# Loading pair 0's q on another queue, moving constant fills off VectorE, and reordering one FFN tile in a fused attention + FFN kernel

## The chip, the cores and the metric

The kernel runs on one core of one Trainium2 chip. The metric is the device time of that core in microseconds (us), from runs without the profiler unless a profiled run is named. The span in a profile is 1.7 to 1.8 us shorter than the time of the same execution.

## The reference

```python
# q, k, v: [8, 8, 576, 64]; x = attention out, [4608, 512]; d_ff = 1536
q_d, k_d, v_d = mean of q, k, v over groups of 4 positions        # 144 positions
out_up    = repeat(softmax(q_d k_d^T / 8) v_d, 4)                 # coarse, upsampled
out_local = softmax(q k^T / 8 where |i - j| < 4) v                # banded
x   = (out_up + out_local).transpose(0, 2, 1, 3).reshape(4608, 512)
out = (relu(x @ w_gate) * (x @ w_val)) @ w_out
```

## The kernel before

The program walks through 32 *pairs* of heads. For a pair it transposes q and k, computes scores (`emit_s1`), takes the exponential on ScalarE, multiplies by the band masks on VectorE, multiplies with v, and writes the normed result, transposed, into `xT`. Four *lead-in* pairs (0 to 3) come first, because the FFN contracts over four pairs. Then 36 *slots* follow: each does one third of an FFN chunk's hidden tiles (`emit_h`) and, for as long as there are any, one more pair. TensorE runs dummy matmuls (`emit_warm`) where it would otherwise stand still in the lead-in.

Constant fills, all on VectorE ahead of its other work:

```python
    nc.vector.memset(zero_sb, 0.0)
    nc.vector.memset(ones_sb[:, 0:64], 1.0)
    nc.vector.memset(ones_sb[:, 64:128], 4.0)
    for t in vw:                                   # 7 buffers, 112 x 768 each
        nc.vector.memset(t[:, :, 64:128], 1.0)
    for t in vd:
        nc.vector.memset(t[:, :, 64:128], 4.0)
    # ... then small fills of qkT (4), ee (2), ed (2), xo (3)
```

The loads of the first nine pairs go through GpSimd's queue and change fp32 into fp16 on the way:

```python
        for src, dst in ((q, qk16[r][:, 0, :]), (k, qk16[r][:, 1, :])):
            if hp < NTP:
                nc.gpsimd.dma_start(dst..., _dap(src, off, ...))
```

The transposes of pairs 0 to 8 are 24 small matmuls into three PSUM banks, q's 12 first, k's 12 after. ScalarE copies the first two banks out, VectorE the third:

```python
        for n in range(2 * NB):                    # 0..5: q, 6..11: k
            bank = b0 if n < 4 else b1 + n // 4 - 1
            for hh in range(2):
                nc.tensor.matmul(out=ps[64 * hh : 64 * hh + 64, bank, lo : lo + 120],
                                 lhsT=sv[:, n // NB, hh, n % NB, :], rhs=eyesum_sb, ...)
        for i, bank in enumerate((b0, b1, b1 + 1)):
            if i < 2:
                nc.scalar.copy(...)                # pooled part, then full part
            else:
                nc.vector.tensor_copy(...)
```

The mask product and the x sum have both inputs in SBUF; so have the additions on GpSimd that pool v over four positions, needed from pair 9 on:

```python
            nc.vector.tensor_tensor(out=o, in0=o, in1=masks..., op=ALU.mult)     # emit_s1
        nc.vector.tensor_tensor(out=xT[...], in0=x[...], in1=x[...], op=ALU.add) # emit_xsum
        nc.gpsimd.tensor_tensor(out=m, in0=t[...], in1=t[...], op=ALU.add)       # emit_vd_pool
        nc.gpsimd.tensor_tensor(out=o..., in0=m[...], in1=m[...], op=ALU.add)    # emit_vd_pool
```

The first FFN slot and the order of a slot's first steps:

```python
    def emit_slot(s, gate):
        c, jj, hp = s // 4, 3 * (s % 4), s + LEAD
        if NVP <= hp + 1 < NP:
            emit_vd_pool(hp + 1)                   # GpSimd, from slot 4 on
        emit_in(hp + 4)                            # GpSimd issues loads
        # ...
        if s == 0:
            emit_qkT_pe(hp, 2, 3)
            emit_warm(2)
            emit_x_pe(hp - 1, 0)                   # pair 3's x into xT
            emit_warm(1)
        # ... then emit_h(c, jj, 0): eight matmuls over all four pairs of xT
```

And the head of the program:

```python
        nc.sync.dma_start(cst_sb, cst_dr)          # masks, identity and so on
        for hp in range(4):
            emit_in(hp)
        emit_warm(10)
        emit_qkT_pe(0, 2, 3)
        emit_warm(4)
        for hp in range(LEAD):
            emit_fill(hp)
```

The softmax here doesn't subtract the row's maximum and nothing guards it: scores larger than these inputs give would overflow.

## Time and profile before

| | before |
|---|---|
| time, median of 3 runs | 358.13 us (358.11 to 358.15) |
| span of the profiled execution | 357.1 us (its time was 358.89, 0.8 above the timed ones) |
| TensorE busy | 349.9 us, 98% |
| q / k of pair 0 land | 5.50 / 6.44 us |
| first exponential | 9.36 us |

The page's first part gives busy time, share and number of instructions of each engine.

```profile
PE 349.9 (98%) x2855; PEld 178.5 (50%) x2855; DVE 227.3 (64%) x338; ACT 212.4 (59%) x366; POOL 187.7 (53%) x231
```

TensorE has next to no idle time to give. The view by stretch shows where the little is; its columns are the length of the stretch, then each engine's busy time with its instruction count, TensorE's granted clock, DMA share and GB/s.

```profile
0.00:10.00 10.00, 8.21 (x61) 3.73 (x62) 7.27 (x26) 3.16 (x7) 8.91 (x14) 1.00 1.58 128
10.00:27.00 17.00, 15.86 (x294) 11.24 (x293) 15.04 (x37) 12.27 (x33) 13.92 (x17) 1.00 2.12 170
```

"Busy" is padded by dummy matmuls, so the lead-in can still be shortened. The timeline of the first 14 us says how. Columns: start, duration, engine, line, operation, output<-input, shapes, count, and in brackets how long the engine stood idle before and what ended that.

```profile
1.26 4.45 PE L557 MATMUL ps<-zero_sb 128*128 128x512 f16 x10 [1.26 <-DVE zero_sb L130]
...
5.63 1.66 PE L214 MATMUL ps<-cst_sb,qk_0_75 96*64 96x120 f16 x24
...
6.30 0.70 DVE L134 MEMSET vw_95<- 112x768 f16 x1
...
7.22 1.04 PE L557 MATMUL ps<-zero_sb 128*128 128x512 f16 x4
...
8.09 0.17 DVE L144 MEMSET xo_111<- 32x128 uint32 x1
8.28 0.26 DVE L229 CAST qkd_100<-ps 128x96 f16<-128x96 f32 x1
...
8.46 0.55 DVE L230 CAST qkT_96<-ps 128x384 f16<-128x384 f32 x1
...
9.36 1.19 ACT L283 ACTIVATE ee_102<-ps 112x576 f16<-112x576 f32 x2 [1.81 <-PE ps L274]
```

VectorE is still filling constants until 8.25 us. The last transposes of pair 0 end at 7.29, but the copies of the third bank do not start before 8.28.

The same view around slot 0:

```profile
25.38 0.61 PE L557 MATMUL ps<-zero_sb 128*128 128x512 f16 x2
...
25.98 0.28 PE L444 MATMUL ps<-cst_sb,xo_109 72*128 72x288 f16 x1
...
26.48 0.38 PE L557 MATMUL ps<-zero_sb 128*128 128x512 f16 x1
...
26.88 1.02 PE L468 MATMUL ps<-xT,wg_sb 128*128 128x512 f16 x4
```

Three dummies surround pair 3's x transposes; then come the eight matmuls of the first hidden tile, until 28.7.

### The profile page before, as it was taken

What the parts mean: (1) busy time and instruction counts of PE and PEld (TensorE: products, weight loads), DVE (VectorE), ACT (ScalarE), POOL (GpSimd) and SP (SyncE); (2) the same over time, 40 slices, a digit from 0 to 9 for tenths busy, and PEclk for the clock granted to TensorE, in tenths of its full rate; (3) what the DMA queues carried; (4) which work ended last, traced back from release to release, by engine and by line L of the source; (5) the groups of instructions that cost most, each with busy time, mean ns of one, the idle gap of its engine ahead of it and who ended that gap; (6) DMA issues with size and microseconds to landing.
All of it is one profiled execution on the core that took longest, in us unless ns stands there. A gap on an engine that the chain in (4) does not pass through costs nothing.

```text
span 357.1 us, 7235 instructions
## 1 busy us (share of the span) xinstructions
PE 349.9 (98%) x2855; PEld 178.5 (50%) x2855; DVE 227.3 (64%) x338; ACT 212.4 (59%) x366; POOL 187.7 (53%) x231
## 2 busy tenths in 40 slices
PE   8999999999999999999999999999999999999996
PEld 3665555545455455555555555554445444444443
DVE  8793666586786877788887788776675432232220
ACT  2766776667777666666666666666776532322321
POOL 8976547999999877767678877722000000000000
PEclk9999999999999999999999999999999999999999
DMA  9999999999999999999999999950000110000022
GB/s 125 165 172 187 182 194 155 166 159 178 169 173 138 159 169 130 132 132 131 133 125 130 124 123 133 117 108 28 21 20 23 44 46 30 31 29 29 31 59 89
DMA packets 166882, 40.11 MB, mean 112 GB/s; under 512 B 149728, under 2 KB 162240, under 8 KB 166848
## 3 DMA queue, kind: packets, MB, share of 16 engines
q0 software_dynamic: 134128, 23.07, 85.8%
q1 hardware_dynamic: 27520, 7.27, 16.2%
q10 hardware_dynamic: 5200, 9.31, 7.7%
q8 instruction: 22, 0.36, 0.4%
q14 instruction: 12, 0.10, 0.1%
HBM read 46.45 MB, written 9.44 MB: 157 GB/s over the span
## 4 chain that ended last, share of the span: by engine, by line
PE 90%; DVE 5%; ACT 2%; issue 1%; DVEq 0%
PE ps L468 51%; PE ps L490 25%; PE ps L408 3%; PE ps L274 2%; PE ps L416 2%; PE ps L214 2%; PE ps L263 2%; DVE xn_114 L386 1%; PE ps L520 1%; ACT rden_112 L385 1%; ACT rden_112 L383 1%; DVE xT L391 1%; PE ps L347 1%; PE ps L247 0%; PE ps L317 0%
## 5 line engine op out<-in xcount | busy, mean ns | idle before, releaser
L468 PE MATMUL ps<-xT,wg_sb 128*128 128x512 f16 x432 | 110.9, 379 | 0.8 <-DVE xn_114 L386 0.5
L468 PE MATMUL ps<-xT,wv_sb 128*128 128x512 f16 x432 | 110.9, 379 | 0.0
L490 PE MATMUL ps<-wo_sb,gT 128*128 128x512 f16 x420 | 100.1, 380 | 0.0
L468 PEld LDWEIGHTS <-wv_sb 128*128 128x128 f16 x432 | 42.2, 98 | 51.1
L468 PEld LDWEIGHTS <-wg_sb 128*128 128x128 f16 x432 | 39.8, 97 | 44.3 <-issue 1.0
L490 PEld LDWEIGHTS <-gT 128*128 128x128 f16 x420 | 39.0, 98 | 45.6
L498 ACT COPY y_sb<-ps 128x512 f32<-128x512 f32 x35 | 20.5, 587 | 46.9 <-PE ps L490 46.9
L432 DVE TENSOR_TENSOR xn_115<-ps,rden_113 64x720 f16<-64x720 f32 x24 | 21.7, 905 | 22.4 <-ACT rden_113 L429 22.1
L432 DVE TENSOR_TENSOR xn_114<-ps,rden_112 64x720 f16<-64x720 f32 x22 | 19.9, 905 | 20.1 <-ACT rden_112 L429 19.8
L283 ACT ACTIVATE ee_102<-ps 112x576 f16<-112x576 f32 x32 | 19.1, 648 | 14.6 <-PE ps L274 14.0
L283 ACT ACTIVATE ee_103<-ps 112x576 f16<-112x576 f32 x32 | 19.1, 648 | 12.5 <-PE ps L274 12.3
L426 ACT ACTIVATE rden_113<-ps 64x720 f32<-64x720 f32 x24 | 18.4, 765 | 7.1 <-PE ps L416 6.8
L286 DVE TENSOR_TENSOR ee_102<-ee_102,cst_sb 112x576 f16<-112x576 f16 x32 | 20.7, 682 | 2.6 <-ACT ee_102 L283 2.4
L426 ACT ACTIVATE rden_112<-ps 64x720 f32<-64x720 f32 x22 | 16.8, 764 | 6.2 <-PE ps L416 5.9
L286 DVE TENSOR_TENSOR ee_103<-ee_103,cst_sb 112x576 f16<-112x576 f16 x32 | 18.4, 615 | 0.0
L391 DVE TENSOR_TENSOR xT<-xn_114 128x576 f16<-128x576 f16 x14 | 13.0, 932 | 0.1
L557 PE MATMUL ps<-zero_sb 128*128 128x512 f16 x33 | 11.4, 457 | 1.3 <-DVE zero_sb L130 1.3
L391 DVE TENSOR_TENSOR xT<-xn_115 128x576 f16<-128x576 f16 x14 | 11.1, 795 | 0.1
L292 ACT ACTIVATE ed_104<-ps 72x576 f16<-72x576 f32 x16 | 10.3, 643 | 0.0
L292 ACT ACTIVATE ed_105<-ps 72x576 f16<-72x576 f32 x16 | 10.3, 643 | 0.0
L429 ACT ACTIVATE rden_113<-rden_113 128x720 f32<-128x720 f32 x12 | 9.6, 803 | 0.4
L235 POOL TENSOR_TENSOR vd_106<-v_0_87 72x256 f16<-72x256 f32 x4 | 2.9, 720 | 12.2 <-PE ps L416 12.1
(463 smaller groups left out, 602.4 us busy)
## 6 DMA issues: line engine op xcount, KB each, us to landing
out_dram<-y_sb ACTq DMA_DIRECT2D x34, 256.0 KB, 4.0
wg_sb<-in_moe_w_gate_dram POOLq DMA_DIRECT2D x4, 384.0 KB, 10.0
wv_sb<-in_moe_w_val_dram POOLq DMA_DIRECT2D x4, 384.0 KB, 10.4
wo_sb<-in_moe_w_out_dram POOLq DMA_DIRECT2D x4, 384.0 KB, 11.8
vw_90<-in_v_dram POOLq DMA_DIRECT2D x5, 168.0 KB, 6.0
vw_91<-in_v_dram POOLq DMA_DIRECT2D x5, 168.0 KB, 5.9
vw_92<-in_v_dram POOLq DMA_DIRECT2D x5, 168.0 KB, 6.6
v_4_86<-in_v_dram POOLq DMA_DIRECT2D x5, 144.0 KB, 7.2
```

The costliest lines, as they stand in the source:

```text
L283: nc.scalar.activation(out=o, in_=ps[0:WK, p0 + 2 * g : p0 + 2 * g + 2, 0:288], func=AF.Exp, scale=scale)
L286: nc.vector.tensor_tensor(out=o, in0=o, in1=_sap(masks_sb, (0, WK), 288 * g, [[0, 2], [1, 288]]), op=ALU.mult,)
L292: nc.scalar.activation(out=ed[r2][:, :, 0 : 2 * SD].rearrange("p h (c t) -> p c h t", c=2), in_=ps[0:72, p0 : p0 + 4, 288:432].rearrange(" ...
L391: nc.vector.tensor_tensor(out=xT[:, kk, b * S : (b + 1) * S].rearrange("p (c t f) -> p c t f", c=2, f=4), in0=x[:, :, 0:288].rearrange("p ...
L408: nc.tensor.matmul(out=ps[:, bank, NQ * j : NQ * j + NQ], lhsT=vflat[:, v0 : v0 + 128], rhs=e[:, hh, lo : lo + NQ], start=True, stop=True,)
L426: nc.scalar.activation(out=r[lo : lo + 64], in_=ps[de : de + 64, 4 + 2 * hh : 6 + 2 * hh, 0:360], func=AF.Ln)
L429: nc.scalar.activation(out=r, in_=r, func=AF.Exp, scale=-1.0)
L432: nc.vector.tensor_tensor(out=x[lo : lo + 64], in0=ps[lo : lo + 64, 4 + 2 * hh : 6 + 2 * hh, 0:360], in1=r[lo : lo + 64], op=ALU.mult,)
L468: nc.tensor.matmul(out=h, lhsT=w[:, kk, bass.ts(jj, 128)], rhs=xT[:, kk, c * TCH : (c + 1) * TCH], start=(kk == 0), stop=(kk == 3),)
L490: nc.tensor.matmul(out=y_ps, lhsT=gts[c, jj][:, bass.ts(ty, 128)], rhs=wo_sb[:, jj, :], start=(jj == 0), stop=(jj == NJJ - 1),)
L498: nc.scalar.copy(out=y_sb, in_=y_ps)
L557: nc.tensor.matmul(out=ps[:, 7, :], lhsT=zero_sb[:, 0:128], rhs=zero_sb[:, 128:640], start=True, stop=True)
```

## The change

There are three intents. (a) Load pair 0's q as fp32 through SyncE's queue and cast it on ScalarE, so that k can take q's place in GpSimd's queue, and transpose k first. (b) Take fills out of VectorE's way: three `vw` fills to GpSimd, the small ones behind the first copies. (c) In slot 0 replace the dummies with the part of the first hidden tile that needs only pairs 0 to 2, and give that slot other PSUM banks.

```diff
@@ -130,18 +131,20 @@
     nc.vector.memset(zero_sb, 0.0)
     nc.vector.memset(ones_sb[:, 0:64], 1.0)
     nc.vector.memset(ones_sb[:, 64:128], 4.0)
-    for t in vw:
+    for t in vw[0:4]:
         nc.vector.memset(t[:, :, 64:128], 1.0)
-    for t in vd:
-        nc.vector.memset(t[:, :, 64:128], 4.0)
     for t in qkT:
 ...
-    for t in ed:
-        nc.vector.memset(t[:, :, 2 * SD :], 0.0)
-    for t in xo:
-        nc.vector.memset(t[64:96, NB:, :], 0.0)
+
+    def emit_pads():
+        for t in ee:
+            nc.vector.memset(t[:, :, S:], 0.0)
+        for t in ed:
+            nc.vector.memset(t[:, :, 2 * SD :], 0.0)
+        for t in vd:
+            nc.vector.memset(t[:, :, 64:128], 4.0)
+        for t in xo:
+            nc.vector.memset(t[64:96, NB:, :], 0.0)
 
     def pair(i):
         return ps[:, 2 * i : 2 * i + 2, :]
@@ -154,7 +157,13 @@
         r = hp % NL
         b, off = head_off(hp)
         for src, dst in ((q, qk16[r][:, 0, :]), (k, qk16[r][:, 1, :])):
-            if hp < NTP:
+            if hp == 0 and src is q:
+                nc.sync.dma_start(
+                    q32.rearrange("p (n d) -> p n d", d=64),
+                    _dap(src, off, [[D, 96], [NQ * D, 2 * NB], [1, D]]),
+                )
+                nc.scalar.copy(out=dst, in_=q32)
+            elif hp < NTP:
                 nc.gpsimd.dma_start(
@@ -207,7 +216,10 @@
     def emit_qkT_pe(hp, b0, b1):
         r, r4, r2 = hp % NL, hp % 4, hp % 2
         sv = qk16[r].rearrange("p i (h j d) -> p i h j d", h=2, d=64)
-        for n in range(2 * NB):
+        blocks = list(range(2 * NB))
+        if hp == 0:
+            blocks = blocks[NB:] + blocks[:NB]
+        for n in blocks:
 ...
@@ -220,14 +232,18 @@
                 )
         big = qkT[r4][:, 0 : 2 * S].rearrange("p (b n t) -> p b n t", b=3, n=4)
         sml = qkd[r2].rearrange("p i t -> p (i t)").rearrange("p (b n t) -> p b n t", b=3, n=4)
-        for i, bank in enumerate((b0, b1, b1 + 1)):
+        act, dve = nc.scalar.copy, nc.vector.tensor_copy
+        if hp == 0:
+            plan = ((2, 1, act), (2, 0, act), (1, 1, dve), (1, 0, dve), (0, 1, act), (0, 0, dve))
+        else:
+            plan = ((0, 1, act), (0, 0, act), (1, 1, act), (1, 0, act), (2, 1, dve), (2, 0, dve))
+        for i, pooled, copy in plan:
+            bank = b0 if i == 0 else b1 + i - 1
             t = ps[:, bank, 0:480].rearrange("p (n t) -> p n t", n=4)
-            if i < 2:
-                nc.scalar.copy(out=sml[:, i], in_=t[:, :, 96:120])
-                nc.scalar.copy(out=big[:, i], in_=t[:, :, 0:96])
+            if pooled:
+                copy(out=sml[:, i], in_=t[:, :, 96:120])
             else:
-                nc.vector.tensor_copy(out=sml[:, i], in_=t[:, :, 96:120])
-                nc.vector.tensor_copy(out=big[:, i], in_=t[:, :, 0:96])
+                copy(out=big[:, i], in_=t[:, :, 0:96])
 
     def emit_vd_pool(hp):
         t, m, o = v4[hp % NV4], v2[hp % 2], vd[hp % 3]
@@ -461,17 +477,21 @@
 
     gts = {}
 
-    def emit_h(c, jj, pp):
+    def emit_h_mm(c, jj, pp, which, kks):
+        w = (wg_sb, wv_sb)[which]
+        for kk in kks:
+            nc.tensor.matmul(
+                out=pair(pp)[:, which, :],
+                lhsT=w[:, kk, bass.ts(jj, 128)],
+                rhs=xT[:, kk, c * TCH : (c + 1) * TCH],
+                start=(kk == 0),
+                stop=(kk == 3),
+            )
+
+    def emit_h(c, jj, pp, parts=((0, range(4)), (1, range(4)))):
         h1, h2 = pair(pp)[:, 0, :], pair(pp)[:, 1, :]
-        for w, h in ((wg_sb, h1), (wv_sb, h2)):
-            for kk in range(4):
-                nc.tensor.matmul(
-                    out=h,
-                    lhsT=w[:, kk, bass.ts(jj, 128)],
-                    rhs=xT[:, kk, c * TCH : (c + 1) * TCH],
-                    start=(kk == 0),
-                    stop=(kk == 3),
-                )
+        for which, kks in parts:
+            emit_h_mm(c, jj, pp, which, kks)
 
         def gate():
             r1 = ffn.tile([128, TCH], FP16, name="r1", tag="r1")
@@ -545,6 +565,8 @@
     def emit_in(hp):
         if hp >= NP:
             return
+        if 4 <= hp < NL:
+            nc.gpsimd.memset(vw[hp][:, :, 64:128], 1.0)
         emit_load(hp)
         if hp in after_load:
             emit_wslice(after_load[hp])
@@ -581,10 +603,16 @@
             emit_qkT(hp + 3)
         if s == 0:
             emit_qkT_pe(hp, 2, 3)
-            emit_warm(2)
+            emit_h_mm(c, jj, 3, 1, range(3))
+            emit_h_mm(c, jj, 3, 0, range(1))
             emit_x_pe(hp - 1, 0)
-            emit_warm(1)
-        elif s <= 5:
+            emit_h(c, jj, 3, ((0, range(1, 4)), (1, range(3, 4))))()
+            emit_s1(hp, 2)
+            emit_h(c, jj + 1, 0)()
+            emit_vd(hp, 6)
+            emit_qkT_pe(hp + 1, 2, 3)
+            return emit_h(c, jj + 2, 3)
+        if s <= 5:
             if s == 5:
                 emit_pool(hp)
             emit_s2t(hp - 1, gate)
@@ -623,11 +651,13 @@
         return emit_h(c, jj + 2, 3)
 
     with tc.manual_schedule(engines={ET.PE, ET.DVE, ET.Activation, ET.SP, ET.Pool}):
+        emit_in(0)
         nc.sync.dma_start(cst_sb, cst_dr)
-        for hp in range(4):
+        for hp in range(1, 4):
             emit_in(hp)
         emit_warm(10)
         emit_qkT_pe(0, 2, 3)
+        emit_pads()
         emit_warm(4)
         for hp in range(LEAD):
             emit_fill(hp)
```

## The prediction

> **What bounds the kernel now.** TensorE: busy 349.9 of 357.1 us (98%) on the page, clock 1.0. By stretch it is busy for all of 100–300 us; of its 7.2 us of idle time 1.8 lie before 10 us, 1.1 in 10–27, 0.8 in 27–60, 3.2 at the tail. The start's busy figure is padding: 33 warm-up matmuls take 11.4 us (groups). So only the first 29 us can be shortened, and what they lose should reach the end one for one.
>
> **The start (chain of waits).** VectorE runs fills from 0.88 to 8.25 us: seven `vw` fills (0.81 apart), then about 1.25 us of small ones. The first transposes' inputs come earlier: q lands at 5.5 (issue 1.28 + 4.2), k at 6.4 (2.32 + 4.1); they end near 7.2. But the third bank's copies are VectorE's: 8.28–9.02. Scores resume at 9.06, the first exp at 9.36. Four fills of 3.97 us follow, chained through transposes, sums, VectorE norming and x transposes.
>
> **What the change does.**
> 1. Three `vw` fills (2.4 us) and 1.1 us of pads leave VectorE before its first copies; it would be free near 4.8. Then the data decide. k takes q's queue place: 5.5–6.3 (estimate from q's 5.5, plus sharing). q on SyncE should be in and cast before. The Trainium skill (DMA: Bandwidth & Descriptors, "Issuing engines are not separate DMA queues") says such transfers share 16 engines, so no extra bandwidth; but the DMA view shows them partly idle until 3 us, and a load (1 us at 140 GB/s) moves there. 24 transposes (0.58 per 12) end at 6.8–7.5, VectorE's three last copies (0.26 + 0.47 + 0.47) at 8.0–8.7. Gain at the first exp 0.4–1.0 us, middle 0.75.
> 2. GpSimd gets three `vw` fills, 0.7–1 us each (estimate from VectorE's 0.70), and loses one DMA issue (1.0). From 17 us it waits for DMA completions anyway: off the chain. Nearest deadline: k of pair 4, landed 23.8, used 24.6.
> 3. Three warm-ups (0.54 + 0.22) beside the last x transposes give way to four of the h tile's eight matmuls, which need only earlier pairs (weights landed by 21.9). Before: 25.45 to 28.76, 3.3 us. After: 8 × 0.23 + 0.66 + up to 0.1 waiting for the last x copy (0.46, covered by two matmuls, 0.46) = 2.6. Gain 0.7.
> 4. Slot 0's new banks keep about 0.5 us between the exps' end (30.84) and the next transposes (31.36): no new wait of note.
>
> 1 and 3 lie wholly on the critical path; later loads land some 10 us before use and absorb nothing.
>
> **Predicted time:** 358.13 − 0.75 − 0.7 = 356.6 us, 80% range 355.7 to 357.5. Chances: faster by over 2% 0.01; within 2% 0.98; slower by over 2% 0.01.
>
> **Right or wrong in the profile.** First exp at 8.4–9.0, no VectorE fill just before the first copies; first transposes at 5.6–6.4, released by k's DMA; h matmuls ahead of pair 3's x transposes; first h done near 27.3, not 28.76; all later work 1.4–1.5 us earlier.
>
> **What would make it wrong.** k landing late because q's and the constants' transfers share the engines (gain 1 gone); q's issue on SyncE taking over 1 us and holding the constants back; TensorE waiting near 23.8 for pair 4's k; GpSimd fills far slower than VectorE's; a wait on the last x copy; or more gain, if the data land before 5.5.

## More of the kernel before

One more stretch, which I did not look at before predicting: slot 5.

```profile
72.09 1.90 DVE L391 TENSOR_TENSOR xT<-xn_114 128x576 f16<-128x576 f16 x1
...
72.20 1.16 POOL L234 TENSOR_TENSOR v_0_87<-v_0_82 72x512 f32<-72x512 f16 x1
...
73.92 1.34 DVE L286 TENSOR_TENSOR ee_103<-ee_103,cst_sb 112x576 f16<-112x576 f16 x2
...
74.94 0.29 PE L408 MATMUL ps<-ee_103,vw_91 112*128 112x96 f16 x3 [0.27 <-DVE ee_103 L286]
```

An x sum takes 1.90 us here; undisturbed it takes 0.76. It lies beside an addition on GpSimd, and TensorE then waits for the mask products.

## The result

| | before | change |
|---|---|---|
| time, median | 358.12 us (358.11 to 358.15, 4 runs) | 358.0 us (357.68, 357.75, 358.26, 359.02) |
| ratio of fast runs | | 1.0001 [0.998, 1.0023] |
| profiled execution | 358.89 (span 357.1) | 357.68 (span 355.9) |

Ratios here and below are the mean time of one kernel's fast runs over that of the other's of the same rounds, with a 95% interval, so they are not quite the ratio of the medians quoted.

The time did not move. The four runs of the change spread by 1.3 us, those of the kernel before by 0.04; but in four of the five later groups single executions of the kernel before took 358.9 to 359.2 us as well, so the spread is not the change's alone. What differs is the lowest time: 358.1 for the kernel before in every group, 357.3 for the change. The two spans must not be compared as they stand, because before's profile is of an execution 0.8 us above its median. A second profile of the unchanged kernel (run before_again, below; 358.11 us, span 356.3) is the fair partner. Below, "shift" is the difference between the start of one matmul in that profile and the start of the same matmul in the other kernel; positive means earlier.

The page's first part of the change, and its stretches:

```profile
PE 347.7 (98%) x2852; PEld 177.8 (50%) x2852; DVE 225.2 (63%) x336; ACT 212.4 (60%) x366; POOL 189.2 (53%) x233
```

```profile
0.00:10.00 10.00, 7.23 (x62) 3.38 (x63) 5.78 (x25) 3.73 (x7) 8.89 (x14) 1.00 1.58 149
10.00:27.00 17.00, 15.88 (x295) 11.26 (x293) 14.72 (x37) 12.02 (x32) 15.29 (x20) 1.00 2.11 170
```

VectorE did lose its fills (7.27 to 5.78 us in the first stretch). TensorE's busy time fell by 1 us there, but that is largely new idle time and fewer half-rate matmuls, not time saved. The timeline of the first 14 us of the change:

```profile
1.27 4.17 PE L579 MATMUL ps<-zero_sb 128*128 128x512 f16 x10 [1.27 <-DVE zero_sb L131]
...
4.11 0.83 ACT L165 CAST qk_0_75<-q_117 96x768 f16<-96x768 f32 x1 [2.08 <-DMA q_117<-in_q_dram]
...
6.63 0.82 PE L226 MATMUL ps<-cst_sb,qk_0_75 96*64 96x120 f16 x24 [1.18 <-DMA qk_0_75<-in_k_dram]
...
7.38 1.04 PE L579 MATMUL ps<-zero_sb 128*128 128x512 f16 x4
7.49 0.26 DVE L244 CAST qkd_100<-ps 128x96 f16<-128x96 f32 x1 [2.81 <-PE ps L226]
...
7.67 1.01 DVE L246 CAST qkT_96<-ps 128x384 f16<-128x384 f32 x2
...
9.15 1.19 ACT L299 ACTIVATE ee_102<-ps 112x576 f16<-112x576 f32 x2 [1.21 <-PE ps L290]
```

q is there early (4.09, cast by 4.94), but all 24 transposes wait for k, which lands at 6.58. TensorE stands still for 1.18 us. VectorE idles 2.81 us and then has three copies to make where it had two. The first exponential comes at 9.15, only 0.21 us earlier.

Slot 0 of the change:

```profile
22.10 0.81 DVE L302 TENSOR_TENSOR ee_103<-ee_103,cst_sb 112x576 f16<-112x576 f16 x2
22.16 0.76 POOL L569 MEMSET vw_95<- 112x768 f16 x1
...
25.18 0.82 PE L483 MATMUL ps<-xT,wv_sb 128*128 128x512 f16 x3
...
26.18 0.28 PE L460 MATMUL ps<-cst_sb,xo_109 72*128 72x288 f16 x1
...
26.68 1.11 PE L483 MATMUL ps<-xT,wg_sb 128*128 128x512 f16 x3
```

Part (c) works as meant: the next pair's scores start at 27.93 instead of 28.70, so the shift there is 0.78, of which 0.57 is slot 0's. GpSimd's fills (0.76 us each) are harmless: a mask product beside one keeps its 0.81 us.

Slot 5 of the change:

```profile
71.32 0.76 DVE L407 TENSOR_TENSOR xT<-xn_114 128x576 f16<-128x576 f16 x1
71.37 1.72 POOL L250 TENSOR_TENSOR v_0_87<-v_0_82 72x512 f32<-72x512 f16 x1
...
72.00 2.31 DVE L302 TENSOR_TENSOR ee_103<-ee_103,cst_sb 112x576 f16<-112x576 f16 x2
...
73.74 0.29 PE L424 MATMUL ps<-ee_103,vw_91 112*128 112x96 f16 x3
...
74.36 0.29 PE L424 MATMUL ps<-ee_103,vw_91 112*128 112x96 f16 x3 [0.26 <-DVE ee_103 L302]
```

and the same stretch of the second profile of the kernel before:

```profile
71.29 1.17 POOL L234 TENSOR_TENSOR v<-v 72x512 f32<-72x512 f16 x1
...
72.10 0.99 DVE L391 TENSOR_TENSOR xT<-xn 128x576 f16<-128x576 f16 x1
...
73.01 1.34 DVE L286 TENSOR_TENSOR ee<-ee,cst_sb 112x576 f16<-112x576 f16 x2
...
74.52 0.29 PE L408 MATMUL ps<-ee,vw 112*128 112x96 f16 x3
...
74.72 0.29 PE L408 MATMUL ps<-ee,vw 112*128 112x96 f16 x3
```

In the change VectorE arrives 0.78 us earlier, but GpSimd does its additions at the same time as before (71.37 against 71.29). The mask products now lie beside them and take 2.31 us instead of 1.34. The first of the weighted sums that read them is still 0.78 us early (73.74 against 74.52), but the next waits for the second mask product and starts at 74.36 instead of 74.72. Of the 0.78 us, 0.42 are given back here: the shift is 0.36 from then to the end, and the spans (356.3 against 355.9) agree.

The Trainium skill says (SBUF — State Buffer, "Who interferes with whom") that a VectorE instruction with two SBUF inputs contends with a GpSimd instruction that reads SBUF, not with one that only writes it. Traces agree on both counts: the two mask products take 0.82 us undisturbed, up to 2.31 beside additions, and 0.81 beside a fill. Counted over the 19 usable traces, 249 of the 251 single mask products that started while an addition was running took over 0.52 us (median 1.41); none of the 35 beside a fill did, and none of the 426 beside no GpSimd work.

That leaves three questions: why the start gained only 0.2, why the change's executions spread, and whether slot 5 is the cause of what is lost later.

### The profile page after: what moved, and what is told of

Same layout as the page of the kernel before. It is cut to its first block, busy times and chain, and to the rows that moved or that the text cites. A ratio compares the mean times of both kernels' runs of the same rounds, so it can differ in the third digit from the quotient of the medians.

```text
span 355.9 us, 7231 instructions
## 1 busy us (share of the span) xinstructions
PE 347.7 (98%) x2852; PEld 177.8 (50%) x2852; DVE 225.2 (63%) x336; ACT 212.4 (60%) x366; POOL 189.2 (53%) x233
## 4 chain that ended last, share of the span: by engine, by line
PE 91%; DVE 4%; ACT 3%; DMA 1%; issue 1%; DVEq 0%; POOLq 0%
PE ps L483 51%; PE ps L510 25%; PE ps L424 3%; PE ps L226 2%; PE ps L290 2%; PE ps L279 2%; PE ps L432 2%; DMA qk_0_75<-in_k_dram 1%; DVE xn_114 L402 1%; PE ps L540 1%; ACT rden_112 L399 1%; DVE ee_103 L302 1%; ACT rden_112 L401 1%; PE ps L363 1%; PE ps L263 0%
## 5 line engine op out<-in xcount | busy, mean ns | idle before, releaser
L302 DVE TENSOR_TENSOR ee_103<-ee_103,cst_sb 112x576 f16<-112x576 f16 x32 | 21.3, 706 | 0.0
L302 DVE TENSOR_TENSOR ee_102<-ee_102,cst_sb 112x576 f16<-112x576 f16 x32 | 19.3, 637 | 1.3 <-ACT ee_102 L299 1.1
L579 PE MATMUL ps<-zero_sb 128*128 128x512 f16 x30 | 10.2, 453 | 1.3 <-DVE zero_sb L131 1.3
L407 DVE TENSOR_TENSOR xT<-xn_115 128x576 f16<-128x576 f16 x14 | 11.3, 807 | 0.1
L407 DVE TENSOR_TENSOR xT<-xn_114 128x576 f16<-128x576 f16 x14 | 11.1, 789 | 0.1
```

The lines of the kernel that those rows point to most:

```text
L302: nc.vector.tensor_tensor(out=o, in0=o, in1=_sap(masks_sb, (0, WK), 288 * g, [[0, 2], [1, 288]]), op=ALU.mult,)
L407: nc.vector.tensor_tensor(out=xT[:, kk, b * S : (b + 1) * S].rearrange("p (c t f) -> p c t f", c=2, f=4), in0=x[:, :, 0:288].rearrange("p ...
L579: nc.tensor.matmul(out=ps[:, 7, :], lhsT=zero_sb[:, 0:128], rhs=zero_sb[:, 128:640], start=True, stop=True)
```

## The experiments

My theory after the first reading was that the start gains little because the loads share bandwidth and k comes late, and that slot 5 gives part back. One rival was that part (c) does not gain what it seems to; a second that the start is worth more, or less, in other executions than in the one profiled; a third, formed later, that the order of the transposes, not the loads, lengthens the start.

Kernels are described by their edit against the change, unless "before" is named. Runs of one group shared a chip and the runs of the kernel before.

| run | this, median (range), us | before, median | ratio [95%] | profiled execution | shift at 60 / 80 us |
|---|---|---|---|---|---|
| after_again | 357.93 (357.31–358.19) | 358.3 | 0.9984 [0.9972, 0.9996] | 357.98 | +0.93 / +0.19 |
| before_again | 358.43 (358.11–359.19) | 358.3 | 1.0008 [0.9996, 1.002] | 358.11 | 0 / 0 |
| slot0_only | 357.85 (357.8–358.66) | 358.3 | 0.9992 [0.998, 1.0004] | 357.81 | +0.69 / +0.31 |
| start_only | 359.05 (358.11–360.11) | 358.3 | 1.002 [1.0002, 1.0037] | 358.16 | −0.11 / −0.11 |
| after_defer | 358.36 (357.33–358.58) | 358.13 | 1.0001 [0.999, 1.0013] | 358.58 | −0.52 / −0.52 |
| before_defer | 358.47 (358.14–358.79) | 358.13 | 1.0007 [0.9994, 1.002] | 358.79 | +0.01 / −0.65 |
| fills_slot0 | 356.27 (356.2–357.32) | 358.13 | 0.9954 [0.9942, 0.9966] | 356.35 | +1.76 / +1.76 |
| fills_slot0_defer | 358.1 (357.06–360.65) | 358.13 | 1.0005 [0.9982, 1.0029] | 360.65 | +1.44 / −2.53 |
| after_noq | 357.37 (one run, state unknown) | 358.14 | – | 357.37 | +1.45 / +0.75 |
| after_warm13 | 357.76 (356.86–358.04) | 358.14 | 0.9983 [0.9971, 0.9995] | 356.86 | +1.19 / +1.19 |
| after_defer5 | 357.6 (357.03–358.34), and one of 918.83 | 358.14 | 0.9982 [0.9969, 0.9995] | 918.83, not used | – |
| fills_slot0_defer5 | 356.58 (356.5–356.62) | 358.14 | 0.9954 [0.9941, 0.9967] | 356.52 | +1.71 / +1.70 |
| after_third | 358.06 (357.95–359.09) | 358.18 | 0.9999 [0.9987, 1.0011] | 359.09 | −0.72 / −1.01 |
| after_warm0 | 358.91 (358.72–359.26) | 358.18 | 1.0019 [1.0005, 1.0034] | 358.81 | −0.75 / −0.75 |
| after_defer5_b | 357.75 (356.72–359.49) | 358.18 | 0.9992 [0.9969, 1.0016] | 359.44 | −0.95 / −1.39 |
| after_warm13_defer5 | 357.19 (357.04–357.52) | 358.2 | 0.9972 [0.9957, 0.9986] | 357.04 | +1.03 / +1.03 |
| after_qfirst | 357.45 (356.65–357.76) | 358.14 | 0.9968 [0.9952, 0.9984] | 357.45 | +1.39 / +0.63 |
| after_qfirst_defer5 | 356.65 (356.43–357.12) | 358.14 | 0.9951 [0.9935, 0.9968] | 356.58 | +1.47 / +1.47 |

Shifts are exact for the profiled execution alone. A kernel's other executions may have started or collided differently, and only their times are known.

### First group: the change and its halves

**after_again** and **before_again** have no edit: they are second profiles of both kernels.

> The changed kernel once more, unedited. Its four runs so far lie between 357.68 and 359.02 us, while the four of the kernel before lie within 0.04. Theory A (the start is now paced by k's landing, which varies from execution to execution): the spread of about 1 us comes again, and the profile shows the first transposes released by k's DMA at a moment other than 6.63 us, with the shift at 28 us (0.76 before) changed by the same amount. Theory B (the later collisions of GpSimd adds with VectorE instructions that have two SBUF inputs fall differently from execution to execution): the spread comes again, but the first transposes start within 0.1 us of 6.63 and the differences arise between 60 and 130 us. Median about 358.0.

> The kernel before, unedited, for a second profile. Its first profile belongs to an execution of 358.89 us, 0.8 above its timed runs. If that profile was a slow sample, this one has a span near 356.3 instead of 357.1, the 0.8 lie in places that a comparison of the two traces shows, and the times stay within 0.1 us of 358.12. Theory A also says: VectorE's fills set the start, so the scores of pair 0 resume within 0.1 us of 9.06 in both profiles.

The second profile of the change begins like the first (first exponential 9.00, shift 0.93 at 60 us) and loses 0.74 us at 74 us, in slot 5 again: this time its x sum lies beside the addition (2.03 us instead of 0.76). Another 0.1 goes between 90 and 130 us. The second profile of the kernel before came out at its floor, 358.11, and became the yardstick. Its times did not stay within 0.1 us as I had expected: they reach 359.19. Against the yardstick, the first profile of before loses 0.6 us in slot 5 and another 0.2 after 120 us. So the loss in slot 5 is no product of the change. What the change does is to arrive there earlier.

**slot0_only**: before, with part (c) alone.

```diff
-            emit_warm(2)
+            emit_h_mm(c, jj, 3, 1, range(3))
+            emit_h_mm(c, jj, 3, 0, range(1))
             emit_x_pe(hp - 1, 0)
-            emit_warm(1)
+            emit_h(c, jj, 3, ((0, range(1, 4)), (1, range(3, 4))))()
+            # and the rest of part (c)
```

> Only the first h tile of the change (four of its matmuls in place of three warm-ups); the start as in the kernel before. From the profile this step gave 0.55 us (3.31 to 2.76 us between the end of the transposes of pair 4 and the end of the first h tile). Theory A: 357.6 us, as tight as the kernel before (within 0.1). Theory B: the shift changes the collisions, so anything from 357.3 to 358.3, and a spread of over 0.3.

The start is that of before (first exponential 9.36), and slot 0 gains 0.69 us: the predicted 0.7. Then slot 5 takes 0.38 of it. The rival that (c) gains less than it seems falls; the prediction's "absorb nothing" falls with it.

**start_only**: the change with the slot 0 of before, so parts (a) and (b) alone.

```diff
-            emit_h_mm(c, jj, 3, 1, range(3))
-            emit_h_mm(c, jj, 3, 0, range(1))
+            emit_warm(2)
             emit_x_pe(hp - 1, 0)
-            emit_h(c, jj, 3, ((0, range(1, 4)), (1, range(3, 4))))()
-            # ...
+            emit_warm(1)
```

> Only the start of the change (q by SyncE, k first, the fills moved); the first h tile as in the kernel before. From the profile the start gave 0.2 us (first exp 9.15 against 9.36). Theory A: median 357.9 to 358.5 with a spread of 0.5 us or more between fast runs. Theory B: 357.9 with whatever spread the later collisions give.

The first exponential comes at 9.07, a gain of 0.29. The shift holds at +0.31 until 26 us, where 0.41 is lost: VectorE begins norming pair 3 only after the second group of sums instead of after the first, and TensorE waits 0.39 us for it. Why VectorE begins there later is open; the same delay is in the profiled change, where part (c) hides all but about 0.1 us of it (0.57 gained instead of 0.69). As a kernel it is 0.2% slower than before, and its times reach 360.11.

### Second group: order on GpSimd, and the change without its loads

**after_defer** and **before_defer** move GpSimd's additions behind the issue of the slot's loads, in every slot, in the change and in before:

```diff
     def emit_slot(s, gate):
         c, jj, hp = s // 4, 3 * (s % 4), s + LEAD
+        emit_in(hp + 4)
         if NVP <= hp + 1 < NP:
             emit_vd_pool(hp + 1)
-        emit_in(hp + 4)
```

> The change, with GpSimd's adds (the pooled sums of v) put behind the loads of the same slot instead of ahead of them, so that in slot 5 they run at about 76 to 78 us instead of 71.3 to 73.7. Theory 1 (GpSimd gate: VectorE's sum into xT and its mask products, which read two operands from SBUF, stand still while GpSimd adds; GpSimd's time is set by its loads and does not move with TensorE, so what the start gained is given back in slot 5): the sum takes 0.76 us and each mask product about 0.45, the wait before the first weighted sums of slot 5 (74 us) is gone, the shift against the kernel before is the same at 80 us as at 60 us (0.8 to 0.95), and the time is 357.2 us with few runs over 357.5. Theory 2 (VectorE is late in slot 5 through its own queue): the wait of 0.3 to 0.4 stays and the time is 357.9. Theory 3 (the spread comes from k's landing): spread of 1 us stays.

> The kernel before with the same move of GpSimd's adds behind the loads. Theory 1: TensorE comes to slot 5 later here, when the adds are nearly over, so the floor stays 358.1 us, and runs above 358.4 (which the kernel before shows on some executions) become rare. Theory 2: no difference from the kernel before in median and spread.

The 357.2 that I expected of after_defer did not come. Its trace loses nothing in slot 5: the additions lie at 69.6 to 71.5 and the x sum and mask products take 0.76 and 0.82 us. But its shift is −0.52 throughout, because its start went badly (first exponential 10.44). That was new; the third and fourth groups pursue it. In before_defer the additions landed on the x sum by accident (72.26 beside 72.09, 1.95 us), and it lost 0.65 there: the same collision, in a kernel with nothing of the change in it. Its slow runs did not become rare, as I had expected, either: the median is 358.47. So moving the additions moves the collision; whether it helps depends on where they fall.

**fills_slot0** is the change without part (a): both loads through GpSimd as before, constants first, q's transposes first, the old assignment of copies.

```diff
-            if hp == 0 and src is q:
-                nc.sync.dma_start(q32..., _dap(src, off, ...))
-                nc.scalar.copy(out=dst, in_=q32)
-            elif hp < NTP:
+            if hp < NTP:
-        blocks = list(range(2 * NB))
-        if hp == 0:
-            blocks = blocks[NB:] + blocks[:NB]
-        # and the copy plan of hp == 0
-        emit_in(0)
         nc.sync.dma_start(cst_sb, cst_dr)
-        for hp in range(1, 4):
+        for hp in range(4):
```

> The change without its load part: q and k of pair 0 both by GpSimd in the old order, the old order of transposes and copies, the constants first; the fills moved and the first h tile as in the change. Since VectorE is free from 4.7 us and q lands at 5.5 and k at 6.4 as in the kernel before, its third-bank copies should end near 7.8 and the first exp start at 8.0 to 8.5, against 9.0 to 9.15 in the change and 9.36 before: a shift of 1.1 to 1.7 us at 60 us, if pair 1's k (10.3) does not hold it to about 1.3. Theory 1: most of it is given back at 74 us, time 357.7 to 358.2. Theory 2 or 3: 356.8 to 357.2.

This is the best kernel: 356.27 us, 0.5% under before, four of its five times within 0.15 us. Its first exponential comes at 8.17, 1.19 us before that of before. Its mask products lie at 71.0 to 71.8, ahead of the additions at 72.5, so slot 5 takes nothing. There is luck in that: in this execution GpSimd waited 1.06 us for a load of k before it came to the additions, which begin at 71.2 to 71.5 in six other traces. Parts (b) and (c) alone gain more than was predicted for the whole, and more than either theory had expected; part (a) costs about 0.8 to 1.0 us in the change's better executions (shift 1.76 against 0.78 and 0.93).

**fills_slot0_defer** adds the deferral in every slot.

```diff
+        emit_in(hp + 4)
         if NVP <= hp + 1 < NP:
             emit_vd_pool(hp + 1)
-        emit_in(hp + 4)
```

> The one before with GpSimd's adds behind the loads of their slot. Theory 1: nothing is given back; 358.1 - 1.3 = 356.8 us (356.5 to 357.1), the fastest of the four. Theory 2: as the one before, within 0.2 us.

A miss. The profiled execution took 360.65: with the additions so late, TensorE waited 2.1 us for the pooled v of a pair. After that wait it ran at half rate for 3.4 us (76.8 to 80.2; the granted-clock column reads 0.50 for 78 to 80, and matmuls of 512 columns start 0.43 us apart instead of 0.22), which cost another 1.5 us. Deferring everywhere is too much; from here on I deferred in slot 5 alone.

### Third group: what the start waits for

**after_noq** sets pair 0's q to zero by a fill instead of loading it. This is wrong (the output still passed the tolerance of the comparison, because pair 0 is a small part of it and its scores are small).

```diff
-                nc.sync.dma_start(
-                    q32.rearrange("p (n d) -> p n d", d=64),
-                    _dap(src, off, [[D, 96], [NQ * D, 2 * NB], [1, D]]),
-                )
+                nc.vector.memset(q32, 0.0)
                 nc.scalar.copy(out=dst, in_=q32)
```

> Wrong result on purpose: the change without q's DMA on SyncE for pair 0 (its buffer is filled with zeros by VectorE instead). If k lands late in the change (5.2 us after its issue, where q took 4.2 in the same place of the queue before) because q and the constants share the 16 DMA engines with it, k's transposes start at 5.4 to 5.8 us here, instead of 6.5 to 6.8. If k's own queue takes that long, they start at 6.5 as before.

Without q's transfer k landed at 5.54 us, 4.25 after its issue. With it, k lands at 5.94 to 7.14 over eleven traces (6.44 to 6.82 in the change's three). The Trainium skill says (DMA: Bandwidth & Descriptors, "Issuing engines are not separate DMA queues") that transfers started by different engines end up on the same 16 DMA engines and interleave; the 1 us that k loses to a transfer on another queue agrees. The constants, which SyncE issues behind q, land at 3.86 without q and at 5.92 with it, so k then shares the engines with both; the run does not separate the two. So issuing q on SyncE buys q 1.4 us (4.09 against 5.50), and k, now first in GpSimd's queue, comes no earlier than it did in second place (6.58 against 6.44).

**after_warm13** gives TensorE three more dummies before the transposes.

```diff
-        emit_warm(10)
+        emit_warm(13)
```

> The change with 13 instead of 10 warm-up matmuls ahead of the first transposes. Clock theory (in the change TensorE stands idle for 0.5 to 1.2 us while it waits for k, so that in some executions the transposes and the four warm-ups behind them still run at half rate, 0.43 instead of 0.22 us per 512 columns, and pair 0's scores resume about 1.3 us later): TensorE is busy until 5.9 to 6.8 us, the transposes take 0.84 us and the four warm-ups 1.04, the first exp starts at 9.0 to 9.3, and no execution is over 358.2 us (357.2 to 358.2, the rest being the slot 5 collision). If the slow executions have another cause, some are above 358.3 as before.

The gap before the transposes shrinks from 1.2 to 0.36 us, but k also landed earlier in this execution (6.17), so the shift of 1.19 is not the dummies' alone. The best time of the change's family up to then (356.86) is this profiled one, which lost nothing in slot 5 (GpSimd waited 1.49 us for a load, and its first addition came at 73.05, after the mask products); the other four lie at 357.6 to 358.0.

**after_defer5** defers the additions in slot 5 only.

```diff
-        if NVP <= hp + 1 < NP:
+        if NVP <= hp + 1 < NP and s != 5:
             emit_vd_pool(hp + 1)
         emit_in(hp + 4)
+        if s == 5:
+            emit_vd_pool(hp + 1)
```

> The change, with GpSimd's adds moved behind the loads in slot 5 alone (the earlier move of all slots let the adds of slot 4 slip into slot 5 instead). Slot gate theory (VectorE's xT sum and masks stand still while GpSimd adds): the sum of slot 5 takes 0.76 us and the two masks 0.82 together, TensorE does not wait before the weighted sums of slot 5, and the shift against the second profile of the kernel before is the same at 80 us as at 60 us (0.78 to 0.95 if the start is of the fast kind, -0.5 if it is of the slow kind with half-rate warm-ups). Fast executions 357.2 us. If VectorE is late for another reason, 0.4 to 0.8 us are lost at 74 us as before.

The profiled execution took 918.83 us with 830 ns per matmul instead of 379; it says nothing of the change and nothing explains it. The other five have a median of 357.6 and still spread by 1.3 us. It was repeated below.

**fills_slot0_defer5** adds the same edit to fills_slot0.

> Fills moved and first h tile as in the change, the loads of pair 0 as in the kernel before, and GpSimd's adds of slot 5 behind its loads. The version of this without the last move ran 356.2 to 357.3 us and met no collision in its profile. Slot gate theory: floor 356.2 again, and the slow execution (357.3) either vanishes (it was a collision) or stays (it was the clock at the start). No gain in the floor.

356.58 with five times within 0.12 us. The ratio equals that of fills_slot0 (0.9954): the median is 0.3 us higher, but there is no outlier such as the 357.32 there. The profiled start was 0.18 us later (first exponential 8.35), the shift 0.06 us less.

### Fourth group: the half-rate start

**after_third** has no edit. It is a third look at the change, to see whether its start varies.

> The change, unedited, for a third profile. Fast start: first exp at 9.0 to 9.15, shift at 60 us 0.78 to 0.93, and 0.4 to 0.75 of it lost at 74 us where the adds meet the xT sum or the masks; time 357.3 to 358.0. Slow start: first exp at 10.2 to 10.5, shift -0.5 at 60 us, nothing lost at 74 us; time 358.4 or more. Median near 358.0.

It does. This execution took 359.09 us and its first exponential came at 10.64, 1.3 us *later* than in the kernel before:

```profile
6.86 1.41 PE L226 MATMUL ps<-cst_sb,qk 96*64 96x120 f16 x24 [1.15 <-DMA qk<-in_k_dram]
...
8.21 1.89 PE L579 MATMUL ps<-zero_sb 128*128 128x512 f16 x4
...
10.02 0.33 PE L279 MATMUL ps<-qkd 64*72 64x144 f16 x2
...
10.64 1.19 ACT L299 ACTIVATE ee<-ps 112x576 f16<-112x576 f32 x2 [2.17 <-PE ps L290]
```

Against the profiled change above, 24 transposes take 1.41 us instead of 0.82 and four dummies 1.89 instead of 1.04. Same instructions, half the rate: the dummies start 0.43 us apart instead of 0.22. The first scores stand behind the dummies in TensorE's queue, so all of it is on the path. The Trainium skill (TensorE: Matmul & The Clock Gate, "Part 1: The HAM clock gate") has it that TensorE runs at half rate until it has been busy for about 3.4 us, as seen by a window that runs freely and so differs from run to run. That agrees: 0.43 becomes 0.22, in some executions by 6.5 us and in others not by 10, after ten dummies of 4.45 us and an idle gap of 1.15. The granted-clock column does not show it, because it counts the time before the trace's first clock record as full; the stretch of 0 to 10 us of the same execution reads 1.00:

```profile
0.00:10.00 10.00, 7.59 (x38) 2.97 (x38) 5.05 (x21) 2.88 (x5) 8.89 (x14) 1.00 1.59 150
```

That first record itself, in the packed trace, agrees with the spacing of the matmuls: full clock is granted from 10.64 us on in this execution, from 10.13 and 10.61 in after_defer and after_defer5_b, and from 5.03 and 5.71 in the first two profiles of the change.

Of the six usable profiled executions that have the change's start and its ten dummies, three stayed at half rate through the start: this one, after_defer and after_defer5_b, with first exponentials at 10.44 to 10.88. A fourth, start_only, changed over within its transposes, at 7.1 us. The kernel before has the half rate too, and hides it: in all four traces of that start q's 12 transposes take 0.71 to 0.82 us instead of 0.51, and the first exponential still comes at 9.36, because VectorE's fills keep the third bank waiting up to 8.28. So part (b) also took away what covered a cold TensorE.

**after_warm0** takes the ten dummies away, so that TensorE is certainly at half rate when k lands.

```diff
-        emit_warm(10)
         emit_qkT_pe(0, 2, 3)
```

> The change without the ten warm-up matmuls ahead of the first transposes, so that TensorE is surely at half rate there. Clock theory: k's transposes start at 6.5 to 6.8, all 24 take about 1.4 us instead of 0.84, the four warm-ups behind them about 1.8 instead of 1.04, the first exp starts at 10.2 to 10.5 instead of 9.0 to 9.15; at 60 us the kernel is 0.4 to 0.6 us behind the second profile of the kernel before, as after_defer was, and the times are 358.3 to 359.3. If the half rate is not what costs, the first exp is at 9.0 to 9.3 and the time 357.9.

The start comes out as in after_third: transposes in 1.41 us, dummies in 1.89, first exponential at 10.35, and 358.91 us. The half rate is therefore enough to produce the change's slow executions; made on purpose it costs 1.2 to 1.35 us at the first exponential against the good starts (9.00 and 9.15).

**after_defer5_b** is after_defer5 again.

> The same kernel as after_defer5, again, since that profile fell on an execution of 918 us. Slot gate theory: in slot 5 the xT sum takes 0.76 us and the masks 0.82 together, no wait of TensorE before the weighted sums, the shift against the second profile of the kernel before equal within 0.1 us at 60 and 80 us. Times: 357.0 to 357.2 for executions with a fast start, up to 358.5 for those with a half-rate start; nothing in between from collisions in slot 5. If the gate theory is wrong, 0.4 to 0.8 us are lost at 74 us all the same.

The profile caught a half-rate start (k at 7.14, first exponential 10.88, shift −0.95). In slot 5 nothing was lost, as the deferral should have it. The times did not fall into the two groups expected: 357.56 and 357.95 lie between, 359.49 above. And 0.43 us went in slot 4, where an x sum took 1.60 us while GpSimd was issuing loads (its addition began only as the sum ended); after_third lost 0.29 at the same place (1.45 us). Over the 19 usable traces this goes with one kind of issue: of the 85 x sums that had the issue of a `vw` load and no addition beside their first 0.75 us, 34 took over 0.85 us; beside other issues alone it was 1 of 96, beside no GpSimd work none of 128. Why some are slowed and others not is open.

**after_warm13_defer5** combines the two repairs.

> The change with 13 warm-ups ahead of the first transposes and with GpSimd's adds of slot 5 behind its loads. If the half-rate start and the slot 5 collision are the two places where the gain goes, the profile has a first exp at 8.7 to 9.2, undisturbed xT sum and masks (0.76 and 0.82 us), the same shift at 60 and 80 us (0.8 to 1.2), and the times are 356.8 to 357.4 us, with few or none above 357.6: about 1.1 us under the kernel before, near the 356.6 that was predicted for the change. If something else takes it, the median stays at 357.7 or above.

357.19 us, with four executions within 0.5 us, where the fourteen of the change lie within 1.8 (357.31 to 359.09). The shift of 1.03 at 60 us is still 1.03 at the end: with the additions deferred to 77.6, the mask products keep their 0.82 us and TensorE does not wait. The share of the deferral does not follow from this run, since after_warm13 kept its shift without it; it follows from the pair after_qfirst and after_qfirst_defer5 below.

```profile
71.07 0.76 DVE L407 TENSOR_TENSOR xT<-xn 128x576 f16<-128x576 f16 x1
...
71.75 0.82 DVE L302 TENSOR_TENSOR ee<-ee,cst_sb 112x576 f16<-112x576 f16 x2
...
77.61 1.16 POOL L250 TENSOR_TENSOR v<-v 72x512 f32<-72x512 f16 x1
```

### Fifth group: loads or order?

Part (a) still cost more than k's landing explains. From k's landing to the first exponential fills_slot0 takes 1.87 us (6.30 to 8.17), the change 2.57 (6.58 to 9.15). In the former q's half of the transposes and ScalarE's first copies are done while k is on its way; in the latter all 24 transposes and three VectorE copies come behind k.

**after_qfirst** keeps the change's loads and restores the order of transposes and copies. **after_qfirst_defer5** adds the deferral in slot 5.

```diff
-        blocks = list(range(2 * NB))
-        if hp == 0:
-            blocks = blocks[NB:] + blocks[:NB]
-        for n in blocks:
+        for n in range(2 * NB):
-        if hp == 0:
-            plan = ((2, 1, act), (2, 0, act), (1, 1, dve), (1, 0, dve), (0, 1, act), (0, 0, dve))
-        else:
-            plan = ((0, 1, act), (0, 0, act), (1, 1, act), (1, 0, act), (2, 1, dve), (2, 0, dve))
+        plan = ((0, 1, act), (0, 0, act), (1, 1, act), (1, 0, act), (2, 1, dve), (2, 0, dve))
```

> The change with the old order of pair 0's transposes (q's blocks first, third bank copied by VectorE last), loads as in the change. From k's landing to the first exp the change takes 2.57 us, the kernel with old loads and old order 1.87. If the order is what lengthens that chain, the first exp comes 1.8 to 2.0 us after k's landing (8.2 to 8.9 for a landing at 6.4 to 7.0), TensorE has q's transposes to do while it waits, and half-rate starts become rarer; shift of the matmuls at 60 us +1.2 to +1.6, time 356.6 to 357.6 depending on slot 5. If only the late landing of k costs, the first exp stays 2.4 us or more after the landing (9.0 or later) and the time stays at 357.9 +- 0.4.

> The same with slot 5's GpSimd adds behind its loads, so that nothing is given back at 74 us. If the order lengthened the chain: 356.4 to 357.0, close to the kernel with old loads and the same deferral (356.58), and a little later than it by k's later landing (0.1 to 0.5 us). If the load of q itself costs more than that: 357.2 or above, as the change with 13 warm-ups and the deferral (357.19).

The order it was: of the transposes, or of the copies, which the same edit puts back; the two are not separated. With k landing at 6.69 and 6.70, later than in the change's first two profiles, the first exponential came at 8.66 and 8.57: 1.97 and 1.87 us after k. From after_qfirst_defer5's timeline:

```profile
6.00 0.51 PE L223 MATMUL ps<-cst_sb,qk 96*64 96x120 f16 x12 [0.29 <-DMA cst_sb<-cst]
...
6.75 0.51 PE L223 MATMUL ps<-cst_sb,qk 96*64 96x120 f16 x12 [0.24 <-DMA qk<-in_k_dram]
...
7.47 0.55 DVE L240 CAST qkT<-ps 128x384 f16<-128x384 f32 x1
...
8.57 1.19 ACT L293 ACTIVATE ee<-ps 112x576 f16<-112x576 f32 x2 [0.87 <-PE ps L284]
```

q's transposes wait for the *constants* (the identity), which SyncE now issues second and which land at 5.96 instead of 3.8; so even here q's early arrival buys nothing. after_qfirst then loses 0.76 us in slot 5 (mask products 2.30 us, beside additions that begin at 71.24), after_qfirst_defer5 loses none. Its 356.65 is 0.1 above fills_slot0_defer5, from a start that is 0.2 us later; the two ratios (0.9951 and 0.9954) do not tell them apart. The 0.98 us between the change's first exponential (9.15) and that of fills_slot0 (8.17) thus splits into 0.28 for k's landing and 0.70 for what lies between landing and exponential.

## Why the prediction was wrong

The prediction was 356.6 us, 1.5 under before: 0.75 for the start, 0.7 for slot 0, and all of it to reach the end. 358.0 was measured. Point by point:

- **"only the first 29 us can be shortened, and what they lose should reach the end one for one"** and **"1 and 3 lie wholly on the critical path; later loads land some 10 us before use and absorb nothing."** This step failed. Loads were the wrong thing to check. In slot 5, VectorE's x sum and mask products meet GpSimd's additions, and GpSimd is paced by its loads, not by TensorE. In the twelve usable traces without a deferral its first addition there starts anywhere from 70.83 to 73.05 us, and not in the order of TensorE's shift: at 71.24 to 71.52 in six whose shifts range from −0.11 to +1.39, at 71.11 with −1.01, at 70.83 with +1.45, at 72.20 with 0.01. The three latest (before, fills_slot0, after_warm13) had waited 0.6, 1.1 and 1.5 us for a load. A TensorE that comes earlier brought VectorE into the additions in five of the seven traces with a shift of over 0.6; that the other two, fills_slot0 and after_warm13, escaped was partly luck. The profiled executions gave back 0.42 and 0.74 (change), 0.38 (slot0_only), 0.70 (after_noq) and 0.76 (after_qfirst). With the additions moved away, nothing is given back: +1.03 and +1.47 stay +1.03 and +1.47 to the end.
- **"Gain at the first exp 0.4–1.0 us, middle 0.75."** Mis-sized. It measured 0.21 and 0.36 in the change's good starts. k landed at 6.4 to 6.8, not at the estimated 5.5 to 6.3, because q's transfer, and the constants that it delays, share the DMA engines with it (5.54 without q). The prediction counted q as a load of 1 us at 140 GB/s, which fits 144 KB; on SyncE it is fp32, 288 KB by the DMA view, and took 3.3 us to land. The larger part is the order: 24 transposes and three VectorE copies behind the last landing, which I had counted but not set against the alternative, 12 transposes and two copies (2.57 us against 1.87).
- **Not foreseen:** the half-rate start. I costed 24 transposes at "0.58 per 12" and did not ask what rate TensorE would be at after standing still for k. In three of six profiles it was at half rate throughout, and the start lost 1.1 to 1.5 us instead of gaining 0.3 (the shift at 60 us less slot 0's 0.57).
- **Right:** slot 0 (0.69 alone; 0.57 within the change), GpSimd's fills (0.76 us each, no effect on the path), the late k as a named risk, and that fills were what VectorE's first copies waited for (fills_slot0 gains 1.19 us at the first exponential).

So the measured sum reads, for the two profiled executions with a good start, 0.21 + 0.57 − 0.42 = 0.36 and 0.36 + 0.57 − 0.74 = 0.19 (0.09 at the end), where 0.75 + 0.7 was predicted; for a half-rate start (after_third) it is −1.29 + 0.57 − 0.29 = −1.01. A mixture of these fits a median of 358.0 with a range of 357.3 to 359.1, but which loss each unprofiled execution had is not known. That the extra dummies and the deferral together bring 357.19, and the old order with the deferral, without extra dummies, 356.65, is shown.

Left open: how the issue of a `vw` load slows an x sum, as in slot 4 of two executions (0.3 to 0.4 us); why VectorE starts norming pair 3 late after the change's start; what happens in the 918 us execution.

## What to carry to other kernels

A gain at the start of a pipelined kernel is only worth what the next fixed-time obstacle lets through: look for engines that keep their own pace (here GpSimd behind its loads) and ask what an earlier TensorE will run into there. When two inputs arrive at different times, do all the work of the first before the second lands, and judge an order by the length of the chain behind the *last* landing; here moving q to another queue left k no earlier than it had been behind q. Ask what rate TensorE runs at after an early wait, and what has covered a slow start so far: with three more dummies ahead of the transposes none of nine executions exceeded 358.04 us. And look at several executions of both kernels before a difference is called the change's.

## What the Trainium skill lacked or had wrong

- TensorE: Matmul & The Clock Gate, Part 1, puts the penalty of the ramp under 1% of a typical kernel's span and advises not to fit a specific count of cold matmuls. The figure holds here: from k's landing to the first exponential the half-rate starts take 1.1 to 1.25 us longer (0.3%). But that is nearly as much as the whole change was meant to gain; the page lacks the warning that a small gain at the start can vanish in it.
- The same page warns in general that the trace's clock events are unreliable. What it lacks is this case of it: the granted clock read 1.00 for 0 to 10 us of an execution whose dummies ran at 0.43 us each instead of 0.22, and 1.0 in one whose matmuls took 830 ns instead of 379 (918.83 us), whose trace holds no clock record at all.
- SBUF — State Buffer, "Who interferes with whom", gives the rule but no size for this pair of instructions. Here an x sum of 0.76 us becomes up to 2.03, and two mask products of 0.82 together become 1.34 to 2.31, beside GpSimd additions of 1.2 to 1.7 us. X sums were also slowed beside the issue of `vw` loads (34 of 85); how was not found.
- DMA: Bandwidth & Descriptors, "Issuing engines are not separate DMA queues", has no figure for how much a second transfer delays a first. Here a load that took 4.25 us from issue to landing beside the constants alone took 5.1 to 5.5 us in the three profiles of the change, with its q load beside it too.
- I found no page that gives a GpSimd fill's time beside VectorE's: 112 x 768 of fp16 took 0.76 us on GpSimd and 0.70 on VectorE.
